# A gated mix of a long convolution and a routed row update on one core: second products of the fine shifts left unsummed, transform differences as accumulating transfers, and a new written-out order

## The chip, the cores and the metric

The kernel runs on one core of one Trainium2 chip. The metric is the device time of one execution in microseconds. An execution is profiled separately; its times are in us from the first instruction unless marked ns. The engines are PE (TensorE matmul; PEld is its weight load), DVE (VectorE), ACT (ScalarE), POOL (GpSimd) and SP (SyncE, which here only issues transfers).

## The reference, cut to what matters

With x of shape (1, 2048, 512) the output is g * a + (1 - g) * b, where g is a sigmoid of one dot product per row.

```python
# a: a long convolution along the 2048 rows, one kernel K per channel
logdA = dt * (A_re + 1j * A_im)                      # 512 channels x 128 states
P = jnp.exp(logdA[:, :, None] * l[None, None, :])    # l = arange(2048) in bfloat16
K = jnp.einsum("dn,dnl,dn->dl", Cc, P, dt * Bc).real
y = irfft(rfft(pad(u)) * rfft(pad(K)))[:2048] + u * Dskip
# b: the two rows of x with the largest x @ w_r go through a small gated MLP,
#    are scaled by a sigmoid and added back to x at their place
```

The lags `l` are rounded to bfloat16, so that far fewer than 2048 different ones occur; the kernel evaluates K at 32 x 20 of them.

## The kernel before, in words

**Lag kernel K.** A lag is written as a coarse part (32 values, `T1`) plus a fine part (20 values, `T2`). For each half `hf` (or `c`) of 256 channels, `coarse(hf)` makes the complex powers exp(logdA * T1), 128 states on the partitions, in tiles `TP`: `phases` makes angles as matmuls on PE (`pa`), ACT turns them to sines and cosines (`sin`), `ns` negates one of them, and two multiplies on DVE (`pi`, `pr`) join them with the decays (`ep`, exponentials on ACT). `fine(hf)` makes the 20 fine powers, weighted by C * dt * B, in `X` (in the region `TQ`): a complex product is two real multiplies, `px` and `py`, and an add, `ps`. For fine shifts 8 to 15 the second products `py` are not added: they lie in `Y`, and PE adds them. For shifts 0 to 7 and 16 to 19 there is a scratch tile (`t4`) and the add `ps` on DVE. `lags(c)` contracts over the states: 64 groups of four channels, each with two parts (real, imaginary); per group and part one matmul of 80 columns (20 shifts x 4 channels, from `X`) and one of 32 columns (8 shifts x 4 channels, from `Y`) into the same PSUM columns 32 to 63 (`kmm`, lines 889 and 890). `kae` copies PSUM to SBUF, `sel` (matmuls of a selection matrix) reorders, `kce`, `kcx` and `k0c` fill `KC`, and `kt` and `ku` make a small tail term. Before these, the weights come from `np` (DVE), `nw` (PE), `kw` (DVE), `wx`, `wp`, `wn`.

**Transforms.** The convolution is done by a cosine and sine transform of each block of 1024 rows. `transform(m)` for block m: for each plane pl (cosine, sine), eight 128x512 products per tile (`fw`), the odd rows first (`fwo`, stored doubled as 2 * odd in V[1]) and then odd plus even (`fwe`, stored in V[0]); `vb` on DVE then makes V[1] = V[0] - V[1], that is even minus odd, one TENSOR_TENSOR of 128x2048 per block and plane. `spectrum(c, i)` makes the transform of K (`ks` on PE, `khe` on ACT). `products(c, j)` multiplies both (`prod`, then `yr`, `yi`, `pq` or PE sums `ac` with `ace`, then `b0` to `b13`), `inverse(c, j)` goes back (`iv` on PE, `ive` on ACT or DVE with the gate as scale, and `out`).

**Rows.** `log` (64 small matmuls on a transposed copy of x, `xt`, loaded by a DMA transpose that occupies SP's queue) gives g and the router's values; `gm`, `gt`, `gm2` find two maxima; `gu` gathers their rows, `ff`, `dn`, `zt`, `z1`, `bu` make the update; `uc` copies x to a DRAM tensor and `sc` scatters the two rows into it; `ue` and `u2` load from there what `inverse` adds. `rd` makes diagonal matrices for that.

**Order.** The program records operations with what they read and write (`P.add`); each may have alternatives on two engines. `PLAN` is a list of (operation number, alternative) written out by hand: it gives every engine its instructions in order, and with them the waits. `BANKS` gives each PSUM tile its bank. An engine runs its list strictly in order. SP's list is a DMA queue; POOL's too, for the few transfers that it issues.

The bookkeeping of buffers matters to the change: a writer waits for all readers of whatever lay at its place before.

## Time and profile before

| what | value |
|---|---|
| time, median of 3 runs | 158.11 us (157.82 to 158.44) |
| time of the profiled execution | 159.26 us, its span 157.2 us |
| mean granted clock of PE | 0.991 |
| busy: PE, DVE, ACT, POOL | 140.8, 137.9, 119.0, 21.0 us |
| instructions: PE, DVE, ACT, POOL | 1622, 184, 177, 26 |
| HBM traffic | 19.78 MB read, 4.20 MB written |

The profiled execution is 2.1 us longer than its span, which is what lies around the first and the last instruction. Engines overlap, so busy times do not add up to the span; what an engine waited for is read from the rows with an idle time before them. The end of a matmul in the profile includes its way through the array, some 0.16 us; the pace of a run of matmuls is read from their starts. A line such as L386 is a helper's (all TENSOR_TENSORs have it); L402 and L408 are PSUM evictions on ACT and DVE, L411 the other ACT functions, L716 is `fw`, L930 and L932 `ks`, L903 `sel`, L1131 `rd`, L618 and L620 the phase products, L548 `nw`, L653 `log`.

### The profile page before, as it was taken

The page shows a single profiled execution, that of the slowest core. Times are in us where ns is not written, and L with a number is a line of the kernel's source. Part 1 is how long each engine was busy: PE and PEld are TensorE (multiplying, and loading weights), DVE is VectorE, ACT ScalarE, POOL GpSimd, SP SyncE. Part 2 cuts the span into 40 slices and gives each one's busy share as a digit, 9 for nine tenths or more (in the row PEclk, how much of TensorE's full clock was granted, in tenths as well). Part 3 has the DMA queues.
Part 4 walks back from the last instruction along what each step waited for, and adds up shares of the span by engine and source line. Part 5 has one row for each costly group of instructions (what it writes and reads, how often), then busy time and mean ns, then how long its engine had stood idle before and what let it go on. Part 6 is the DMA issues. An engine that isn't in the chain of part 4 may idle for free.

```text
span 157.2 us, 3769 instructions
## 1 busy us (share of the span) xinstructions
PE 140.8 (90%) x1622; PEld 103.5 (66%) x1635; DVE 137.9 (88%) x184; ACT 119.0 (76%) x177; POOL 21.0 (13%) x26
## 2 busy tenths in 40 slices
PE   2479998999998999999967999999999999999960
PEld 0259976444764555778636899668877767777850
DVE  0799689999998999999999999999987999996930
ACT  5699999999999898887982754758687963567820
POOL 5000011564508800002020000000000000000000
PEclk9999999999999999999999999999999999999996
DMA  3999999968399000340397500558000040000157
GB/s 84 216 245 272 314 424 409 407 233 254 103 364 559 17 0 4 81 190 1 65 363 259 152 8 4 179 163 264 15 4 0 0 133 0 6 0 0 33 159 212
DMA packets 20932, 24.35 MB, mean 155 GB/s; under 512 B 9358, under 2 KB 18068, under 8 KB 20244
## 3 DMA queue, kind: packets, MB, share of 16 engines
q1 hardware_dynamic: 20642, 23.97, 47.3%
q8 instruction: 13, 0.21, 0.6%
q10 hardware_dynamic: 146, 0.13, 0.3%
q0 software_dynamic: 128, 0.01, 0.2%
q14 instruction: 3, 0.02, 0.0%
HBM read 19.78 MB, written 4.20 MB: 153 GB/s over the span
## 4 chain that ended last, share of the span: by engine, by line
PE 53%; DVE 32%; issue 4%; POOL 3%; ACT 2%; DMA 1%; POOLq 1%; ACTq 0%
DVE RB L386 23%; PE psm L930 9%; PE psm L1076 9%; PE psm L993 5%; PE psm L889 4%; PE psm L995 3%; PE psm L548 3%; PE psm L997 3%; PE psm L932 2%; PE psm L1071 2%; POOL RB L396 2%; PE psm L935 2%; DVE RB L726 2%; DVE RB L408 2%; PE psm L598 2%
## 5 line engine op out<-in xcount | busy, mean ns | idle before, releaser
L386 DVE TENSOR_TENSOR RB<-RB 128x2048 bf16<-128x2048 bf16 (+5 forms) x112 | 110.0, 1033 | 2.4 <-ACT RB L402 1.1
L402 ACT ACTIVATE RB<-psm 128x1024 bf16<-128x1024 f32 (+5 forms) x54 | 49.1, 945 | 23.7 <-PE psm L997 10.0
L716 PE MATMUL psm<-RB 128*128 128x512 bf16 x121 | 28.8, 379 | 1.2 <-ACT RB L402 0.5
L411 ACT ACTIVATE RB<-RB 128x512 bf16<-128x512 f32 (+6 forms) x48 | 27.0, 644 | 1.7 <-DVE RB L386 1.5
L411 ACT ACTIVATE RB<-psm 128x1024 bf16<-128x1024 int16 (+2 forms) x23 | 21.6, 968 | 2.5 <-DVE RB L386 1.2
L716 PEld LDWEIGHTS psm<-RB 128*128 128x128 bf16 x128 | 11.7, 97 | 14.0 <-ACT RB L402 1.1
L1076 PE MATMUL psm<-RB 128*128 128x256 bf16 x128 | 18.9, 273 | 0.0
L889 PE MATMUL psm<-RB 128*128 128x80 bf16 x256 | 16.5, 197 | 0.0
L890 PE MATMUL psm<-RB 128*128 128x32 bf16 x256 | 16.4, 177 | 0.0
L889 PEld LDWEIGHTS psm<-RB 128*128 128x128 bf16 x256 | 16.1, 96 | 0.2
L890 PEld LDWEIGHTS psm<-RB 128*128 128x128 bf16 x256 | 16.0, 96 | 0.2
L930 PE MATMUL psm<-RB 128*128 128x256 bf16 x128 | 14.5, 273 | 1.5 <-ACT RB L402 1.5
L930 PEld LDWEIGHTS psm<-RB 128*128 128x128 bf16 x128 | 12.4, 98 | 3.9 <-ACT RB L402 2.1
L1076 PEld LDWEIGHTS psm<-RB 128*128 128x128 bf16 x128 | 12.5, 98 | 1.5
L408 DVE CAST RB<-psm 128x1024 bf16<-128x1024 f32 (+3 forms) x8 | 8.6, 1080 | 3.7 <-PE psm L548 1.7
L993 PE MATMUL psm<-RB 128*128 128x512 bf16 x35 | 11.3, 379 | 0.3
L1087 ACT ACTIVATE RB<-psm,RB 128x256 bf16<-128x256 f32 x25 | 9.8, 477 | 1.3 <-PE psm L1076 1.1
L396 POOL CAST RB<-RB 128x16 bf16<-128x16 f32 (+4 forms) x6 | 7.2, 1197 | 24.8 <-DVE RB L405 16.9
L618 PE MATMUL psm<-RB 128*128 128x256 f16 x64 | 9.0, 272 | 0.0
L1071 PE MATMUL psm<-RB 128*128 128x256 bf16 x32 | 8.7, 273 | 0.0
L995 PE MATMUL psm<-RB 128*128 128x256 bf16 x40 | 8.3, 272 | 0.1
L997 PE MATMUL psm<-RB 128*128 128x256 bf16 x40 | 8.3, 273 | 0.0
(74 smaller groups left out, 156.9 us busy)
## 6 DMA issues: line engine op xcount, KB each, us to landing
RB<-c_fwd SPq DMA_DIRECT2D x2, 1024.0 KB, 7.9
RB<-in_A_u_dram SPq DMA_DIRECT2D x2, 1024.0 KB, 6.8
RB<-c_near SPq DMA_DIRECT2D x2, 1024.0 KB, 5.2
RB<-u_routed SPq DMA_DIRECT2D x2, 1024.0 KB, 5.1
RB<-in_B_w_up_dram SPq DMA_DIRECT2D x1, 1792.0 KB, 10.4
RB<-in_B_w_gate_dram SPq DMA_DIRECT2D x1, 1792.0 KB, 14.4
RB<-in_B_w_down_dram SPq DMA_DIRECT2D x1, 1792.0 KB, 8.7
out_dram<-RB SPq DMA_DIRECT2D x6, 256.0 KB, 3.0
```

The costliest lines, as they stand in the source:

```text
L386: return P.add(name, [(eng, c_dve(n, mode) if eng == DVE else 1.6, lambda h: h.tensor_tensor(out=o(), in0=a_(), in1=b_(), op=op))], rd, wr ...
L402: return lambda h: h.activation(out=o(), in_=a_(), func=ACTF.Copy, scale=scale() if callable(scale) else scale)
L411: return P.add(name, [(ACT, cost or c_act(n), lambda h: h.activation(out=o(), in_=a_(), func=func, scale=scale))], rd, wr, table=table, **kw)
L716: x = h.matmul(P32(t, k2, 0, 128, 0, (1, 512)), FM(0, 128, pl * 4096 + (par * 4 + i) * 512 + (2 * kp + k2) * 128, (1, 128)), U(0, 128, ((m ...
L889: h.matmul(P32(t, q // 6, 0, 128, (q % 6) * 80, (1, 80)), tp, TQv(0, 128, c * 10240 + ri * NT2 * 256 + r * 4, (256, NT2), (1, 4)), start=( ...
L890: x = h.matmul(P32(t, q // 6, 0, 128, (q % 6) * 80 + 32, (1, 32)), tp, ARENA(0, 128, eY[c] + ri * 2048 + r * 4, (256, 8), (1, 4)), start=F ...
L930: x = h.matmul(o, KN(0, 128, g * 2048 + col, (1, 128)), KC[c](0, 128, g * 256, (1, 256)), start=(g == 0), stop=(g == NG - 1))
L993: r = h.matmul(P32(t, kt, 0, 128, 0, (1, 512)), CI(0, 128, 0, (1, 128)), f(k, 0, 512), start=(k == 0 and hc == 1), stop=False, skip_group_ ...
L995: r = h.matmul(P32(t, kt, 0, 128, 256, (1, 256)), CI(0, 128, 0, (1, 128)), f(k, 0, 256), start=False, stop=False, skip_group_check=True)
L997: r = h.matmul(P32(t, kt, 0, 128, 0, (1, 256)), NEG(0, 128, 0, (1, 128)), f(k, 1, 256), start=False, stop=(k == od[-1]), skip_group_check= ...
L1071: h.matmul(o, RD(0, 128, (tb + 8) % 16 * 128, (1, 128)), UE[q](0, 128, r * 256, (1, 256)) if early else U2(0, 128, tb * D + c * CW, (1, 25 ...
L1076: x = h.matmul(o, G(0, 128, (pl * 2 + kt // 2) * 1024 + (r * 2 + q) * 128, (1, 128)), PQ(0, 128, r * 1024 + kt * 256 + pl * 256 if quarter ...
```

## The change: what it does

1. **`fine`.** The adds `ps` of shifts 4 to 7 and of 16 to 19 are gone. Their second products are written to `Y`, which now holds 16 shifts (4 to 19) in two pieces per part, instead of 8. `py` for shifts 8 to 15 becomes two multiplies of 128x2048 instead of one of 128x4096. The add of shifts 0 to 3 stays.
2. **`lags`.** The second matmul has 64 columns (16 shifts x 4 channels) instead of 32, into PSUM columns 16 to 79.
3. **`transform`.** Odd rows are stored as -2 * odd. `vb` is no longer a DVE instruction: it is two DMAs with accumulation, issued by POOL (`ACC`), that add V[0] to V[1], 128 x 2 x 512 values (256 KB) each; four such pairs in all.
4. **Small things.** `ldt` (log_dt) is loaded from SP's queue, ahead of all, instead of ACT's. The tile `neg` gets a place of its own. In program order `products(0, 0)` and `inverse(0, 0)` come after `lags(1)`.
5. **`PLAN` and `BANKS`** are new. What moves, read from the new list against the old one:

| engine | before | after |
|---|---|---|
| SP, start | cia, ldn, nat1, nat3, nat4, dga, nat5, dsr, nat2, xt, cf, dgb, fm1, u0, fm0 | ldt, cia, nat1, dgb, ldn, dga, nat5, dsr, xt, nat4, nat2, nat3, cf, u0, fm1, fm0 |
| SP, later | kt (half 0), u8, ue, tm, u2, ue, kt (half 1), u2 | u8, ue, ue, u2, kt (half 1), u2, kt (half 0), tm |
| PE, start | phases of qargs0 and weights, nw, log, phases of coarse0 | phases of coarse0, weights, qargs1, qargs0, log, coarse0; nw after the second gt |
| PE, middle | coarse1 phases between fw of both blocks, lags0, sel, four ks, lags1 | the same, with other fw; zt after sel; five ks before lags1 |
| DVE, start | args mixed with np, kw, wx, then rows and gm | all args, log and gm, np between the gm steps, kw after powers |
| DVE, from fine1 on | rest of fine1, vb, vb, prod, prod, yi, kae, vb, yr, pq, kce, ... vb | rest of fine1, prod, bu, prod, yr, yi, kae, pq, pq, kce, khe, ... |
| DVE, new there | | three ns, two khe, rd of block 0 (from ACT); dtn |
| ACT, before sel | ..., neg, ..., k0c, kae, kae, rd, then kcx, kce | ..., kae, kae, k0c, kcx, kce, then rd of block 1 |
| ACT, later | rd of block 1 between ace; last ive of inverse(1,1) on DVE | z1 after four khe; last ive of inverse(1,1) on ACT |
| POOL | ..., sgo, rsf, sgd, sgo, gsil, hh, sc, rr | ..., rr, gsil, hh, sgd, vb (block 0, plane 1), sgo, vb (block 1, plane 1), vb (block 0, plane 0), rsf, vb (block 1, plane 0), sc |

The diff, without the two lists:

```diff
+        def ACC(name, vs, rd, wr, kb):
+            return P.add(name, [(POOL, 1.5 * len(vs), lambda h: [h.dma_start(out=o(), in_=a_(), accum_op=ALU.add) for o, a_ in vs])], rd, wr, dma=(4.0, kb / 100.0, len(vs)))
...
+        NEG, bNEG = small("neg", 256, BF)
...
-        DMA("ldt", ..., eng=ACT, first=2900.0, lat=2.0)
+        DMA("ldt", ..., first=2900.0, lat=2.0)
...
-                    P.add("fwo", [(ACT, c_act(1024), f_act(o, a, 2.0)), (DVE, ... scalar1=2.0 ...)], [t], [bVO[m][pl]])
+                    P.add("fwo", [(ACT, c_act(1024), f_act(o, a, -2.0)), (DVE, ... scalar1=-2.0 ...)], [t], [bVO[m][pl]])
...
-                v = lambda hc, pl=pl: (lambda: V(0, 128, vo[m][0] + (hc * 2 + pl) * 512, (vo[m][2] - vo[m][0], 2), (2048, 2), (1, 512)))
-                TT("vb", v(1), v(0), v(1), ALU.subtract, [bV[m][0][pl], bVO[m][pl]], [bV[m][1][pl]], 2048)
+                v = lambda hc, z, pl=pl: (lambda: V(0, 128, vo[m][2 * z] + (hc * 2 + pl) * 512, (2048, 2), (1, 512)))
+                ACC("vb", [(v(1, z), v(0, z)) for z in range(2)], [bV[m][0][pl], bVO[m][pl]], [bV[m][1][pl]], 512)
...
-        YR = [("V", 16384), ("TQ", 8192)]
+        YR = [((("V", 16384), ("V", 20480)), (("A", 22528), ("S", 2048))), ((("TQ", 8192), ("TQ", 12288)), (("A", 22528), ("TQ", 16384)))]
...
+            y = lambda b_, ri: Y[ri][b_ // 2] + 1024 * (b_ % 2)
+            y2 = lambda b_: ap(y(b_, 0), (y(b_, 1) - y(b_, 0), 2), (256, 4), (1, 256))
             for k, (j0, b0) in enumerate(((0, 4), (4, 0))):
-                bt = bf_("t%d_%d" % (j0, hf), "A", 22528, 4096)
+                bt = bY[hf][0] if k else bf_("t%d_%d" % (j0, hf), "A", 22528, 4096)
+                o_ = y2(0) if k else t4
                 TT("px", x(j0, 4), ...)
-                TT("py", t4, ...)
-                TT("ps", x(j0, 4), x(j0, 4), t4, ALU.add, [bx[k], bt], [bx[k]], 2048)
+                TT("py", o_, ...)
                 if k == 0:
+                    TT("ps", x(j0, 4), x(j0, 4), t4, ALU.add, [bx[k], bt], [bx[k]], 2048)
...
-            TT("py", ap(Y, (2048, 2), (256, 8), (1, 256)), ap(N, (X - N, 2), (0, 8), (1, 256)), ..., [bY[hf]], 4096)
+            for ri in range(2):
+                TT("py", ap(y(1, ri), (y(2, ri) - y(1, ri), 2), (256, 4), (1, 256)), ap(X if ri else N, (0, 8), (1, 256)), ..., [bY[hf][1 + ri]], 2048)
             TT("px", x(16, 4), ...)
-            TT("py", t4, x(0, 4, 1, -5120), ..., [bt], 2048)
-            TT("ps", x(16, 4), x(16, 4), t4, ALU.add, [bx[3], bt], [bx[3]], 2048)
+            TT("py", y2(3), x(0, 4, 1, -5120), ..., [bY[hf][3]], 2048)
...
-                                x = h.matmul(P32(t, q // 6, 0, 128, (q % 6) * 80 + 32, (1, 32)), tp, ARENA(0, 128, eY[c] + ri * 2048 + r * 4, (256, 8), (1, 4)), ...)
+                                x = h.matmul(P32(t, q // 6, 0, 128, (q % 6) * 80 + 16, (1, 64)), tp, ARENA(0, 128, eY[c][ri][0] + r * 4, (eY[c][ri][1] - eY[c][ri][0], 2), (256, 8), (1, 4)), ...)
...
-        inverse(0, 0, products(0, 0))
         fine(1)
         residual(1)
         lags(1)
+        inverse(0, 0, products(0, 0))
```

More of the change, by code (lines that the diff above doesn't have):

```diff
@@ L472, in bass_gated_mix__ssm_conv_s4__moe_arch_mod__prompt_kernel @@
         prm = [A_A_re, A_A_im, A_B_re, A_B_im, A_C_re, A_C_im]
-        DMA("ldt", lambda h: [h.dma_start(LDT(0, 1, 0, (1, D)), dr(A_log_dt, 0, (D, 1), (1, D)))], [], [bLDT], 1, eng=ACT, first=2900.0, lat=2.0)
+        DMA("ldt", lambda h: [h.dma_start(LDT(0, 1, 0, (1, D)), dr(A_log_dt, 0, (D, 1), (1, D)))], [], [bLDT], 1, first=2900.0, lat=2.0)
         DMA("cia", lambda h: [h.dma_start(CI(0, 128, 0, (1, 128)), dr(id_c, 0, (512, 128), (1, 128)))], [], [bCIA], 32, eng=SP, first=2900.0)
@@ L725, in store @@
                 else:
[L726 removed]
+                    P.add("fwo", [(ACT, c_act(1024), f_act(o, a, -2.0)), (DVE, c_dve(1024, 1), lambda h: h.tensor_scalar(out=o(), in0=a(), scalar1=-2.0, scalar2=None, op0=ALU.mult))], [t], [bVO[m][pl]])
             return product, store
```

25 lines of the change are left out of this document (12 added, 13 removed), and 64 rows, old and new, of the table PLAN.

## The prediction

> **What bounds the kernel now.** I read the shares of the engines first, then the busy time by stage, then the chain and single rows. The page's shares of the engines, the chain's shares, and busy time in six stages up to PE's end (stretch, length, busy us and count of PE, PEld, DVE, ACT, POOL, then clock, DMA share, GB/s):
>
> ```profile
> PE 140.8 (90%) x1622; PEld 103.5 (66%) x1635; DVE 137.9 (88%) x184; ACT 119.0 (76%) x177; POOL 21.0 (13%) x26
> PE 53%; DVE 32%; issue 4%; POOL 3%; ACT 2%; DMA 1%; POOLq 1%; ACTq 0%
> 0.00:20.00 20.00, 13.76 (x128) 11.23 (x129) 13.16 (x31) 16.29 (x25) 2.25 (x8) 1.00 0.93 229
> 20.00:65.00 45.00, 42.98 (x393) 25.25 (x398) 43.27 (x64) 43.45 (x61) 16.62 (x17) 1.00 0.63 239
> 65.00:79.40 14.40, 13.38 (x291) 11.19 (x292) 14.19 (x16) 12.27 (x16) 1.73 (x2) 1.00 0.35 109
> 79.40:83.60 4.20, 2.68 (x48) 1.42 (x48) 4.10 (x5) 3.63 (x10) 0.43 (x1) 1.00 1.00 375
> 83.60:114.00 30.40, 30.39 (x473) 25.79 (x474) 29.52 (x27) 18.07 (x21) 0.00 (x0) 1.00 0.40 122
> 114.00:152.00 38.00, 37.66 (x296) 28.64 (x298) 33.00 (x45) 25.30 (x47) 0.00 (x0) 1.00 0.09 26
> ```
>
> The reader is to see that PE, not DVE, has the least room. From 83.60 to 152.00 PE stands still 0.35 us of 68.4. From 20 to 83.6 it stands still 2.02 + 1.02 + 1.52 = 4.6 us, and DVE and ACT are as full as PE there (1.7 and 1.6 us idle in 20 to 65). The change removes no PE work. So it can win only what PE waits for: those 4.9 us, and part of the 6.2 us before 20. The chain's 32% on DVE says that DVE leads somewhere, not that its time is worth as much at the end.
>
> Where DVE hands over to PE (rows of both engines; start, length, then what ended the idle time before):
>
> ```profile
> 60.50 2.29 DVE L386 TENSOR_TENSOR RB<-RB 128x4096 bf16<-128x4096 bf16 x1
> 65.23 0.20 PE L889 MATMUL psm<-RB 128*128 128x80 bf16 x1
> 78.31 0.18 PE L890 MATMUL psm<-RB 128*128 128x32 bf16 x1
> 79.40 2.68 PE L903 MATMUL psm<-RB 128*32 128x128 bf16 x48 [0.91 <-ACT RB L402]
> 79.86 2.45 ACT L1131 ACTIVATE RB<-RB 128x128 bf16<-128x128 bf16 x8 [0.52 <-POOL RB L386]
> 82.34 1.22 ACT L402 ACTIVATE RB<-psm 32x512 bf16<-32x512 f32 x2
> 83.61 0.61 PE L930 MATMUL psm<-RB 128*128 128x256 bf16 x4 [1.53 <-ACT RB L402]
> 87.62 2.29 DVE L386 TENSOR_TENSOR RB<-RB 128x4096 bf16<-128x4096 bf16 x1
> 89.82 2.35 DVE L386 TENSOR_TENSOR RB<-RB 128x2048 bf16<-128x2048 bf16 x2
> 90.61 0.20 PE L889 MATMUL psm<-RB 128*128 128x80 bf16 x1
> ```
>
> The last operand of `lags0` is done at 62.79, PE comes to it at 65.23: 2.4 us spare. The last of `lags1` is done at 89.91, PE comes at 90.61: 0.7 us spare. The two `vb` of `transform0` follow at 89.82.
>
> **The change part by part.**
>
> *Sums dropped in `fine`* (two `ps` per half). Each is a 128x2048 TENSOR_TENSOR as in the row at 89.82, two in 2.35 us, or 1.15 each: 4 x 1.15 = 4.6 us less DVE. Two stand before 62.79, where PE came 2.4 us later anyway; two before 89.91, where it came 0.7 us later. On the end: 0 by themselves. They are the cover for PE coming earlier. Cutting `py` of 4096 in two costs some 0.1 us of DVE per half, covered.
>
> *Differences `vb` as transfers*: another 4.6 us less DVE. The first pair stands behind `fine1`, before the first `prod`; PE has `lags1` and `spectrum0` to do then and waits 0.01 us in that stage. On the end: 0, provided that they land in time (below).
>
> *Wider second product.* 256 matmuls go from 32 to 64 columns:
>
> ```profile
> 66.72 0.60 PE L620 MATMUL psm<-RB 128*128 128x256 f16 x4
> 39.27 1.54 PE L779 MATMUL psm<-RB 128*128 128x2 bf16 x56
> ```
>
> 24 pairs run from 65.23 to 66.72, 62 ns a pair. 56 matmuls of two columns take (1.54 - 0.16)/55 = 25 ns each, so narrow ones pay a floor of 25, and the 80-column partner the other 37. Bounds for 64 columns: 25 (nothing) and 37 (256 x 12 = 3.1 us). A straight line from 25 ns at 32 columns to 37 at 80 gives 33 at 64, or 2.0 us. But 37/80 is 0.46 ns a column, and by that the floor reaches to 54 columns and 64 take 29.6: I take 256 x 4.5 = 1.1 us more, all of it on PE, half before `sel` and half in `lags1`. The Trainium skill (TensorE: Matmul & The Clock Gate, "Wait — 56ns, not 53.3ns?") gives a warm pitch of columns/2.4 GHz + 2.5 ns, never under 25: an estimate of 29.2 ns and 1.1 us in all, against 2.0 by the straight line, which would end at 157.9 instead of 157.0; the trace agrees at 2 columns, no run here shows 64.
>
> *Start.* `ldt` leaves ACT's queue, so A_re is issued first there:
>
> ```profile
> 0.72 0.52 ACTq L473 DMA_DIRECT2D RB<-in_A_log_dt_dram  x1
> 1.27 0.37 ACTq L476 DMA_DIRECT2D RB<-in_A_A_re_dram  x1
> 4.78 9.09 SPq L420 DMA_TRANSPOSE RB<-in_A_u_dram  x1
> RB<-in_A_u_dram SPq DMA_TRANSPOSE x1, 11.2
> 12.52 4.59 PE L548 MATMUL psm<-RB 128*128 128x128 f32 x32
> 15.83 1.28 PE L548 MATMUL psm<-RB 128*128 128x128 f32 x10
> 17.16 2.26 PE L653 MATMUL psm<-RB 128*128 128x2 bf16 x64
> 19.29 0.38 PE L618 MATMUL psm<-RB 128*128 128x256 f16 x2
> 20.59 0.61 PE L599 MATMUL psm<-RB 128*128 128x256 f16 x4
> 17.15 1.23 DVE L408 CAST RB<-psm 128x1024 bf16<-128x1024 f32 x1 [1.70 <-PE psm L548]
> L399 DVE SCALAR_TENSOR_TENSOR RB<-RB 128x256 f32<-128x256 bf16 x8 | 3.6, 477 | 0.0
> ```
>
> A_re comes 0.55 us earlier; A_im stays third on SP, so I take -0.4 for all that hangs on both (bounds 0 and -0.55). The transpose `xt` moves one place up SP (-0.4) and three `nat` loads move behind its 9.09 us. They then land near 18, and so `np` and `nw` move behind `log`. `log` now begins at 4.4 + 11.2 = 15.6 and ends at 17.9 (19.4 before). PE then still owes `nw`: 32 at the pace of its last ten, 0.11 us, 3.6 us (the 4.59 has a slow head). It has done two other phase products instead, 1.3 us each by the stretch from 19.29 to 20.59. So it is 1.5 us earlier with 1.0 us more to do; I take -0.2, since the first products of a cold PE are slow in any order (bounds -0.5 and +0.5). DVE, though, stands from about 12 to 18. By 18.4 it had done eight `np` (3.6 us) and `kw` (1.2); now they come after, and it is some 4 us behind, net of the small row operations that it does first. With two `ps` fewer (2.3) and the start's 0.4 its last operand for `lags0` comes at 62.8 + 4 - 2.3 - 0.4 = 64.1, if its 1.7 us of waits in 20 to 65 stay: still ahead of PE, but by little.
>
> *ACT lighter.* All three `ns` of ACT (1.05 us each) go to DVE, `z1` and one `rd` (2.45) go behind `sel`, the other `rd` to DVE:
>
> ```profile
> L402 ACT ACTIVATE RB<-RB 128x1024 bf16<-128x1024 bf16 x3 | 3.2, 1054 | 0.1
> ACT RB L402 <- PE psm L997: 10.0, 8, 2.4
> ```
>
> In 65 to 83.6 PE waits for ACT (the 0.91 and 1.53 above); before, its waits are many and short, and I take ACT, which empties PSUM, as the likeliest releaser. With 3.2 + 2.5 us less work for it I let PE win 1.3 of the 3.0 us that it stands still in 20 to 79.4 (bounds 0 and -3.0; what brings them back is a rival below). The 0.9 before `sel` and the 1.22 of `kcx` and `kce` after it stay; `rd` ends at 82.31, `sel` at 82.08, so its removal gives -0.2. After `sel` DVE gets `rd` and two `khe`, some 3.5 us; `vb` and `ps` gave it 6.8 there, and ACT's longest wait for PE, 10.0 us in all, shows that ACT had room.
>
> *Products of channel half 0 after `lags1`* in program order: in the old written-out order they already ran about there, so nothing moves by it but the banks. 114 to 152: DVE lighter, -0.2 of the 0.34. `ive` for the last tile on ACT instead of DVE: +0.1.
>
> *The transfers.* On POOL they stand behind `sgd`, in the order transform0 plane 1, transform1 plane 1, transform0 plane 0, `rsf`, transform1 plane 0, then the scatter `sc`. The second waits for ACT's eviction of transform1, in the old run at 67.4, in the new order behind one more sine, near 72; all behind it wait too: plane 0, which the first `prod` (near 89) needs, and `rsf`, which `z1` on ACT needs near 90.
>
> ```profile
> 66.42 1.01 ACT L402 ACTIVATE RB<-psm 128x1024 bf16<-128x1024 f32 x1
> 72.92 1.07 POOL L812 DMA_INDIRECT u_routed<-RB  x1 [18.30 <-DVE RB L386]
> u_routed<-RB POOLq DMA_INDIRECT x1, 4.2
> out_dram<-RB SPq DMA_DIRECT2D x6, 256.0 KB, 3.0
> RB<-RB SPq DMA_DIRECT2D x2, 48.0 KB, 3.5
> L396 POOL CAST RB<-RB 128x1 bf16<-128x1 f32 x1 | 3.3, 3307 | 5.1 <-DVE RB L663 5.1
> 46.69 3.40 DVE L386 TENSOR_TENSOR RB<-RB 128x4096 bf16<-128x4096 bf16 x2
> ```
>
> No row shows an accumulating transfer. Issue: 1.07 us to 3.3 (POOL's slowest row, one element). Landing of 256 KB: 3.0 us to 3.5 x 256/48 = 18.7. Nearest are POOL's own: 1.07 and 4.2. So 72 + 4 x 1.07 + 4.2 = 80.5, 8 us before `prod`: cost 0. The far end, 72 + 13.2 + 18.7 = 104, costs 13 us, since one `kae` of `lags1` stands on DVE behind four of these products and `sel` waits for it: two of 2.29 and two of 1.15 take DVE from 89 to 96, PE's ten groups of 12 pairs (66 ns) take it from about 89.5 to 97.5, so DVE has 1.5 to 2 us to spare, until about 91. `sc` now goes out after `bu` near 92 rather than 73 and lands near 97; on SP's queue `ue` waits for it, and behind `ue` stand `u2`, both `kt`, `tm` and the first `out`. All but `out` land by about 110, and their reader, `iv` of half 0, runs in the last stage, after 114: covered.
>
> **Sum**: start -0.4, order up to `log` -0.2, PE's waits -1.3, `rd` -0.2, width +1.1, last stage -0.2 and +0.1 = -1.1. The profiled execution took 159.26 us for a span of 157.2 (so some 158.2 is due), and the median of the runs shown is 158.11, 1.15 below it; taken off the median: 157.0 us.
>
> **The rivals.**
>
> *Slower: the transfers land late.* What speaks for it: POOL's one-element cast took 3.3 us while DVE ran multiplies for 3.4. If each issue costs 3.3 and the landing doubles to 8.4, plane 0 lands at 72 + 13.2 + 8.4 = 93.6, 2.6 us past 91; from 1.1 us late on it eats the whole gain. It gives 158.11 - 1.1 + 2.6 = 159.6. Against it: the 1.07 us row also lies under a busy DVE. Beside it, the Trainium skill (SBUF — State Buffer, "SBUF: two separate sides") says that a transfer issued by GpSimd has its descriptors written by that engine, which a VectorE instruction in a two-port mode locks out; the 3.3 us row may be of that kind; no run here shows it for a transfer.
>
> *Slower: DVE's idle stretch from 12 to 18.* If the `nat` loads land 2 us past 18, `np` waits, and behind it on DVE every eviction of transform0 that frees a bank for PE's next `fw`; `lags0`, whose last operand comes at 64.1 by the sum above, is late by some 2.5: 158.11 - 1.1 + 2.5 = 159.5. It decides from 1.1 us on. Against it: `cf`, which leaves SP right behind the transpose now, delayed nothing.
>
> *No change*: PE's waits in 20 to 79.4 come back elsewhere: 158.11 - 1.1 + 1.3 = 158.3. For it: DVE and ACT are 96% full there and the order is as tight as before.
>
> *More*: nearly all waits from 20 to 83.6 go, another -1.7 (the rest of the 3.0): 155.3. Against: `kcx` and `kce` still follow `sel`.
>
> **How the numbers follow.** Likeliest 157.0, chance 0.48, its own range 156.0 to 158.0. No change 0.20, more 0.11, late transfers 0.12, early DVE 0.09. A change under 0.5% (0.8 us) can't be told from none here; of the likeliest case's own range some seven tenths lie beyond it. So faster 0.34 + 0.11 = 0.45, same 0.14 + 0.20 = 0.34, slower 0.12 + 0.09 = 0.21. Range 155.0 to 160.0: it takes in every case above; the 18.7 us landing, some 170, lies outside.
>
> **What would show it.** PE's first `kmm` near 64.5 and `sel` near 78; kmm pairs near 66 ns; the first phase product near 8.3; DVE with a gap before `log`, some 128 to 131 us busy, and new gaps after 90; POOL issues near 72 to 77 of about 1 us each. Wrong, if a pair takes over 70 ns, if the first `prod` waits for a DMA, or if PE idles over 3 us between 20 and 65.

## The result and the profile after

The changed kernel takes 157.85 us, median of 20 runs (156.42 to 158.69); the kernel before takes 158.54 beside it, median of 20 (157.82 to 159.66). The ratio is 0.9935, 95% interval 0.9909 to 0.9961: 1.0 us less (0.6 to 1.4). The medians differ by 0.7, the means (157.55 and 158.57) by 1.0, since the runs of the changed kernel lie in two groups. 157.0 was predicted. Runs more than 1.5% above the fastest of their kernel are left out of the ratios, not of the medians. The groups are eight runs from 156.42 to 157.12 and twelve from 157.65 to 158.69 (median 158.02), with nothing between. The profiled execution, 156.56 us with a span of 154.8, is of the lower group, 1.3 us under the median, so its trace is not the typical case; what may part the groups comes below.

The profile after: the shares of the engines, the chain, and busy time by stage (columns as before):

```profile
PE 141.0 (91%) x1635; PEld 103.7 (67%) x1635; DVE 132.9 (86%) x181; ACT 114.1 (74%) x168; POOL 28.7 (19%) x34
...
PE 63%; DVE 25%; DMA 5%; SPq 1%; ACT 1%; issue 1%; ACTq 0%; DVEq 0%
...
0.00:20.00 20.00, 13.51 (x134) 9.93 (x135) 9.64 (x28) 16.32 (x26) 2.68 (x9) 1.00 0.88 222
20.00:65.00 45.00, 44.60 (x443) 27.79 (x441) 44.67 (x66) 42.27 (x60) 14.31 (x16) 1.00 0.80 277
...
79.40:83.60 4.20, 2.66 (x31) 2.15 (x24) 4.20 (x6) 3.71 (x11) 1.03 (x1) 1.00 1.06 283
83.60:114.00 30.40, 30.25 (x464) 24.95 (x462) 27.82 (x27) 19.46 (x22) 2.74 (x1) 1.00 0.48 127
```

PE does the same work (141.0 us against 140.8), DVE 5.0 us less. From 20 to 65 PE stands still 0.40 us, where it stood 2.02. DVE had 1.7 us idle in that stretch and has 0.3 now: the shorter list of DVE was spent at once on an order in which PE arrives earlier.

The hand-overs, in the order of those shown of before (rows of PE, DVE and ACT):

```profile
59.58 3.50 DVE L386 TENSOR_TENSOR RB<-RB 128x2048 bf16<-128x2048 bf16 x3
63.13 0.10 PEld L897 LDWEIGHTS psm<-RB 128*128 128x128 bf16 x1 [0.27 <-DVE RB L386]
74.86 0.19 PE L898 MATMUL psm<-RB 128*128 128x64 bf16 x1
...
75.83 0.19 PE L898 MATMUL psm<-RB 128*128 128x64 bf16 x1
77.09 2.68 PE L911 MATMUL psm<-RB 128*32 128x128 bf16 x48 [1.06 <-ACT RB L402]
80.33 0.95 DVE L408 CAST RB<-psm 128x768 bf16<-128x768 f32 x1
81.53 2.67 PE L938 MATMUL psm<-RB 128*128 128x256 bf16 x23 [1.54 <-DVE RB L408]
89.43 0.20 PE L897 MATMUL psm<-RB 128*128 128x80 bf16 x1
```

`lags0` starts at 63.13 instead of 65.23, and PE now waits for DVE there (before, DVE was 2.4 us early). `sel` starts at 77.09 instead of 79.40. The gap ahead of the spectrum is as long as it was, 1.54, but the releaser is another: `kce` on DVE, which stands behind three operations of `fine1` and starts at 80.33 though `sel` ends at 79.77. Fifteen pairs from 74.86 to 75.83 make 65 ns a pair.

The start, first of the kernel before, then of the changed kernel (ACT's wait for the small load; DVE; PE's phase products; `log`):

```profile
8.71 0.61 PE L598 MATMUL psm<-RB 128*128 128x256 f16 x2 [3.16 <-DVE RB L386]
```

```profile
5.62 3.85 ACT L411 ACTIVATE RB<-RB 128x4 bf16<-128x4 bf16 x8 [2.07 <-DMA RB<-in_A_log_dt_dram]
5.86 0.17 DVE L405 CAST RB<-RB 128x4 f32<-128x4 bf16 x1 [1.04 <-ACT RB L411]
9.05 0.61 PE L622 MATMUL psm<-RB 128*128 128x256 f16 x2 [3.90 <-DVE RB L386]
10.94 0.63 PE L622 MATMUL psm<-RB 128*128 128x256 f16 x2
13.14 0.38 PE L602 MATMUL psm<-RB 128*128 128x256 f16 x2
15.11 2.27 PE L657 MATMUL psm<-RB 128*128 128x2 bf16 x64
17.41 0.19 DVE L405 COPY RB<-psm 128x32 f32<-128x32 f32 x1 [4.93 <-PE psm L657]
```

`dtn` (the CAST at 5.86) now stands on DVE between `al` and `bs`. It waits for `dth` on ACT, that for the load of log_dt, which lands at 5.6; so `bs` and all behind it come later, and the first phase product starts at 9.05, 0.34 later than before. The two rows of the same kind at 10.94 and 13.14 show PE's speed: 0.63 us for two matmuls, then 0.38; start to start these are 213 and 107 ns.

The end (SP's output transfers and the last multiply on an output), before and after:

```profile
149.52 3.96 SPq L1099 DMA_DIRECT2D out_dram<-RB  x4
152.01 0.69 DVE L1091 TENSOR_TENSOR RB<-psm,RB 128x512 bf16<-128x512 f32 x1 [0.51 <-PE psm L1076]
153.52 0.81 SPq L1095 DMA_DIRECT2D out_dram<-RB  x1
```

```profile
150.25 1.22 SPq L1107 DMA_DIRECT2D out_dram<-RB  x2
150.73 0.84 ACT L1095 ACTIVATE RB<-psm,RB 128x256 bf16<-128x256 f32 x2 [2.46 <-PE psm L1084]
151.59 0.56 SPq L1103 DMA_DIRECT2D out_dram<-RB  x1
```

Before, the last output was ready at 152.70 but SP was still issuing four others until 153.48; from the end of the last multiply to the end of the span 4.5 us passed. Now it is issued at once, and 3.2 us pass.

The transfers (group, transfer; the `ns` multiply on DVE, whose mean was 416 ns before):

```profile
L420 POOL DMA_DIRECT2D RB<-RB x8 | 10.3, 2305 | 3.8 <-ACT RB L402 3.8
RB<-RB POOLq DMA_DIRECT2D x8, 256.0 KB, 8.9
L629 DVE TENSOR_SCALAR RB<-RB 128x1024 bf16<-128x1024 bf16 x8 | 4.2, 520 | 0.5 <-ACT RB L411 0.4
```

Eight issues keep POOL busy for 10.3 us, 1.29 each (single rows overlap, hence the mean of 2.3), and a transfer lands 8.9 us after its issue, twice the 4.2 assumed. Still no `prod` waits: the first starts at 89.20, right behind `fine1`.

Another wait for a load is new. `ku` on DVE, a small multiply, reads what `kt` brings (DVE's row):

```profile
108.10 4.83 DVE L386 TENSOR_TENSOR RB<-RB 128x256 bf16<-128x256 bf16 x5 [0.83 <-DMA RB<-RB]
```

DVE has no such wait in the profile before. There the parts of `kt` land 3.4 to 3.6 us after their issue; now they take 3.9 to 5.9. More loads run beside them (the DMA engines' share from 104 to 110 is 0.92, where it was 0.62), but that this is the cause is not shown. DVE also comes to `ku` sooner without the differences; with these back on DVE (below) its profile has no such wait.

### The profile page after: what moved, and what is told of

Read it like the earlier page. It is cut to its first block, busy times and chain, and to the rows that moved or that the text cites. A ratio compares the mean times of both kernels' runs of the same rounds, so it can differ in the third digit from the quotient of the medians.

```text
span 154.8 us, 3775 instructions
## 1 busy us (share of the span) xinstructions
PE 141.0 (91%) x1635; PEld 103.7 (67%) x1635; DVE 132.9 (86%) x181; ACT 114.1 (74%) x168; POOL 28.7 (19%) x34
## 4 chain that ended last, share of the span: by engine, by line
PE 63%; DVE 25%; DMA 5%; SPq 1%; ACT 1%; issue 1%; ACTq 0%; DVEq 0%
DVE RB L386 17%; PE psm L720 17%; PE psm L1084 7%; PE psm L897 5%; PE psm L622 5%; PE psm L938 5%; PE psm L898 4%; PE psm L1001 4%; DMA RB<-RB 3%; DVE RB L399 3%; PE psm L624 3%; DVE RB L408 2%; DMA RB<-in_A_log_dt_dram 2%; PE psm L783 2%; PE psm L911 2%; PE psm L1079 2%
## 5 line engine op out<-in xcount | busy, mean ns | idle before, releaser
L386 DVE TENSOR_TENSOR RB<-RB 128x2048 bf16<-128x2048 bf16 (+7 forms) x106 | 101.0, 1001 | 2.2 <-DMA RB<-RB 0.8
L402 ACT ACTIVATE RB<-psm 128x1024 bf16<-128x1024 f32 (+5 forms) x52 | 47.8, 942 | 25.1 <-PE psm L1005 10.3
L720 PE MATMUL psm<-RB 128*128 128x512 bf16 x128 | 29.3, 379 | 0.0
L720 PEld LDWEIGHTS psm<-RB 128*128 128x128 bf16 x128 | 12.2, 98 | 13.3 <-ACT RB L411 0.2
L1084 PE MATMUL psm<-RB 128*128 128x256 bf16 x128 | 18.9, 273 | 0.0
L897 PEld LDWEIGHTS psm<-RB 128*128 128x128 bf16 x256 | 16.9, 96 | 0.7 <-issue 0.3
L897 PE MATMUL psm<-RB 128*128 128x80 bf16 x256 | 17.4, 198 | 0.0
L898 PE MATMUL psm<-RB 128*128 128x64 bf16 x256 | 17.4, 191 | 0.0
L898 PEld LDWEIGHTS psm<-RB 128*128 128x128 bf16 x256 | 16.9, 97 | 0.0
L938 PE MATMUL psm<-RB 128*128 128x256 bf16 x128 | 14.3, 273 | 1.5 <-DVE RB L408 1.5
L1095 ACT ACTIVATE RB<-psm,RB 128x256 bf16<-128x256 f32 x28 | 11.2, 477 | 5.2 <-PE psm L1084 5.1
L938 PEld LDWEIGHTS psm<-RB 128*128 128x128 bf16 x128 | 12.4, 98 | 3.4 <-issue 1.7
L1084 PEld LDWEIGHTS psm<-RB 128*128 128x128 bf16 x128 | 12.5, 98 | 1.5
L408 DVE CAST RB<-psm 128x1024 bf16<-128x1024 f32 (+3 forms) x10 | 11.0, 1105 | 2.4 <-PE psm L898 1.1
L1001 PE MATMUL psm<-RB 128*128 128x512 bf16 x40 | 12.6, 380 | 0.2
L420 POOL DMA_DIRECT2D RB<-RB x8 | 10.3, 2305 | 3.8 <-ACT RB L402 3.8
L622 PEld LDWEIGHTS psm<-RB 128*128 128x128 f16 x64 | 6.3, 103 | 6.1 <-DVE RB L386 4.4
L1079 PE MATMUL psm<-RB 128*128 128x256 bf16 x32 | 8.7, 273 | 0.0
```

Source lines behind the costliest of these rows:

```text
L386: return P.add(name, [(eng, c_dve(n, mode) if eng == DVE else 1.6, lambda h: h.tensor_tensor(out=o(), in0=a_(), in1=b_(), op=op))], rd, wr ...
L402: return lambda h: h.activation(out=o(), in_=a_(), func=ACTF.Copy, scale=scale() if callable(scale) else scale)
L408: return P.add(name, [(ACT, 0.10 + n * 0.83e-3, f_act(o, a_)), (DVE, 0.15 + n * 1.04e-3, lambda h: h.tensor_copy(o(), a_()))], rd, wr, **kw)
L622: r = h.matmul(o, DGM(0, 128, d * 128, (1, 128)), HL(0, 128, z * 512 + hf * CW, (1, CW)), start=(u == 0 and z == 0 and i % 2 == 0), stop=F ...
L720: x = h.matmul(P32(t, k2, 0, 128, 0, (1, 512)), FM(0, 128, pl * 4096 + (par * 4 + i) * 512 + (2 * kp + k2) * 128, (1, 128)), U(0, 128, ((m ...
L897: h.matmul(P32(t, q // 6, 0, 128, (q % 6) * 80, (1, 80)), tp, TQv(0, 128, c * 10240 + ri * NT2 * 256 + r * 4, (256, NT2), (1, 4)), start=( ...
```

## The experiments

Times of different batches are compared through their ratios to the kernel before, which ran beside each; the half-widths of two ratios are combined as the root of their squares. The upper group of the changed kernel alone lies at 0.9968 of the kernel before (means, 158.07 to 158.57).

**Width alone, in the old order.** In the kernel before, one argument of the second lag product:

```
- ..., 0, 128, (q % 6) * 80 + 32, (1, 32)), tp, ARENA(..., (256, 8), (1, 4))
+ ..., 0, 128, (q % 6) * 80 + 16, (1, 64)), tp, ARENA(..., (0, 2), (256, 8), (1, 4))
```

> The kernel before, with nothing changed but the second product of a lag pair, 64 columns instead of 32 (its 32 columns of `y` read twice, so the lag sums get terms that don't belong). It prices the width alone, in the old order, with all sums still on DVE. Theory (TensorE is the bound from 65 to 83.6 and in lags1, so width is paid in full): pairs go from 62 to 65.4-66.5 ns, 256 pairs cost 0.9 to 1.1 us, the time is 0.6 to 1.3 us above the kernel before. Rival (the waits for DVE and ACT around the lags take the width up): pairs as wide, but the time is within 0.3 us of the kernel before.

Measured: 159.63 us, ratio to the kernel before 1.0058 (1.0026 to 1.0090): 0.9 us more (0.4 to 1.4). The groups of the two lag products, of the kernel before and of this one:

```profile
L889 PE MATMUL psm<-RB 128*128 128x80 bf16 x256 | 16.5, 197 | 0.0
L890 PE MATMUL psm<-RB 128*128 128x32 bf16 x256 | 16.4, 177 | 0.0
```

```profile
L889 PE MATMUL psm<-RB 128*128 128x80 bf16 x256 | 17.4, 198 | 0.0
L890 PE MATMUL psm<-RB 128*128 128x64 bf16 x256 | 17.3, 191 | 0.0
```

The 256 pairs take 17.4 us instead of 16.5. That is the 0.9, and the end moves by all of it: PE is the bound there, as predicted.

**Transfers alone, in the old order.** In the kernel before, `vb` as accumulating transfers (and `fwo` scaled by -2), three of the four behind `hh` on POOL, one behind `rr`:

```
- TT("vb", v(1), v(0), v(1), ALU.subtract, ...)
+ ACC("vb", [(v(1, z), v(0, z)) for z in range(2)], ...)
```

> The kernel before, with nothing changed but the four `vb`: eight accumulating transfers on POOL, in the gaps of POOL's old queue (three of them behind `hh`, so from about 55 us, the fourth behind `rr`). Theory of the prediction (DVE's time there is covered): within 0.3 us of the kernel before; the two `vb` between 89.8 and 92.1 go, the first `prod` starts near 90, and what DVE gains stands as idle time in front of `kae` or later. Rival (DVE leads in lags1 and after, so 2.3 us less ahead of `kae` are worth something): 0.5 to 1.2 us below the kernel before. Second rival (POOL's issues and their hold on the SBUF port cost DVE): 0.5 us or more above it, with DVE's `ns` or `pi` during the issues longer by 0.4 us each.

Measured: 159.14 us, ratio 1.0024 (0.9995 to 1.0052): 0.4 us more (-0.1 to +0.8). DVE loses 4.3 us of work (137.9 to 133.6) and nothing is won. Not as expected, the first `prod` does not start near 90: it waits for ACT (DVE's row of this kernel):

```profile
91.93 5.75 DVE L386 TENSOR_TENSOR RB<-RB 128x4096 bf16<-128x4096 bf16 x3 [2.15 <-ACT RB L402]
```

So in the old order the two `vb` ahead of `prod` filled a wait. They were free there. The second rival is not excluded: the interval reaches past 0.5, and one `ns` on DVE took 0.70 us during the issues, instead of 0.42.

**Differences back on DVE, in the new order.** The changed kernel with the old `vb`, two ahead of the first `prod`, two ahead of the first `prod` of the other half:

```
- ACC("vb", ...)   # POOL, behind sgd
+ TT("vb", v(1), v(0), v(1), ALU.subtract, ...)   # DVE
```

> The changed kernel, with the four differences back on DVE as one subtraction each: transform0's two just ahead of the first `prod`, transform1's two just ahead of the first `prod` of the other channel half. Theory (in the new order DVE has 1.06 us idle before `kae` and 0.8 before `ku`): the first pair pushes `kae` of lags1 by 2.3 - 1.1 = 1.2 us, `sel` of lags1 by about as much, less what ACT holds it for; the time is 0.3 to 1.2 us above the changed kernel. The prediction's pricing of the transfers at nothing would hold with a time within 0.3 us of the changed kernel. Rival (the transfers cost the port and DMA time): below it by 0.3 us or more.

Measured: 159.78 us, ratio 1.0066 (1.0041 to 1.0090); against the changed kernel 1.0066/0.9935 = 1.0132, half-width 0.0036: 2.1 us more (1.5 to 2.6), above the range that I gave. PE's weight loads ahead of `sel` of `lags1` and of the first of the accumulated products:

```profile
100.78 2.16 PEld L911 LDWEIGHTS psm<-RB 128*32 128x32 bf16 x48 [1.67 <-ACT RB L402]
...
116.53 0.13 PEld L1001 LDWEIGHTS psm<-RB 128*128 128x128 bf16 x2 [2.09 <-ACT RB L402]
```

In the changed kernel these loads wait 0.49 and 0.61 us. Both pairs of `vb` push PE, by 1.2 and 1.5 us. The releaser in brackets is the last by the profile; DVE's `kae`, which ends at 100.67 behind the `vb`, is the one that comes later than before. What was free in the old order is not in the new one. All eight runs lie between 159.46 and 160.01; against the upper group of the changed kernel alone they are 1.6 us longer (1.0066/0.9968), still above the range.

**Sums back on DVE, narrow product, in the new order.** The changed kernel with

```
+ TT("ps", x(j0, 4), x(j0, 4), o_, ALU.add, ...)      # for both k
+ TT("ps", x(16, 4), x(16, 4), y2(3), ALU.add, ...)
- second product: 64 columns
+ second product: 32 columns
```

> The changed kernel, with the four `ps` back on DVE and the second product of 32 columns, the same sums as before; order and transfers as in the changed kernel. Theory (dropping the sums was needed as cover for the new order): PE saves 0.9 us of width, but the last operand of lags0 comes 2.3 us later than 63.1 where PE waits already, and lags1's 2.3 us later than 89.3; with 0.45 us of width given back on each side the time is 1.5 to 3.5 us above the changed kernel. Rival (the sums are worth nothing and the width costs): 0.5 to 1.0 us below the changed kernel.

Measured: 162.63 us, ratio 1.0239 (1.0201 to 1.0276); against the changed kernel 1.0306, half-width 0.0046: 4.8 us more (4.1 to 5.6), again above the range. PE's first pair of `lags0` and of `lags1`, and two windows behind the latter:

```profile
66.69 0.21 PE L899 MATMUL psm<-RB 128*128 128x80 bf16 x1 [1.26 <-DVE RB L387]
...
95.00 0.20 PE L899 MATMUL psm<-RB 128*128 128x80 bf16 x1 [2.41 <-DVE RB L387]
...
95.00:98.00 3.00, 3.00 (x78) 3.00 (x79) 3.00 (x3) 0.97 (x1) 0.29 (x1) 0.71 0.02 5
98.00:101.00 3.00, 3.00 (x83) 3.00 (x81) 2.97 (x3) 0.21 (x1) 2.45 (x1) 0.72 0.00 0
```

The restored `ps` show as PE waiting for DVE, and there is more: after the stand of 2.41 us ahead of `lags1` the granted clock is 0.71 and 0.72 in the next two windows. The stand is paid twice: 6 us at that clock lose some 1.7 us of work (an estimate from the two windows).

**Around `sel`.** In the changed kernel's written-out order:

```
- kmm 286, kae 287 | kmm 283, kmm 284, kae 285 | px, ps, kce
+ kmm 283, kmm 284, kae 285 | kmm 286, kae 287 | px, kce, ps
```

> The changed kernel, with two moves around `sel` of lags0: the one-bank group of lag pairs (`kmm` 286, evicted in 0.44 us) goes last instead of the two-bank group (0.97 us), so that the last eviction before `sel` is the short one; and `kce` on DVE goes ahead of one `ps` of fine1. Theory (PE stands still 1.19 us before `sel` for ACT and 1.70 us before `ks` for DVE's `kce`, which is queued behind fine1's operations): the gap before `sel` falls to about 0.7, the one before `ks` to about 1.4, 0.5 to 0.8 us in all, and the time is 0.4 to 0.8 us below the changed kernel, unless fine1's last operand (89.28, PE waits 0.35 for it already) then holds PE. Rival (that one holds: DVE, not PE's gaps, sets when lags1 starts): both gaps shrink, the gap before lags1 grows by as much, and the time is within 0.3 us of the changed kernel.

Measured: 158.37 us, ratio 0.9978 (0.9950 to 1.0005); against the changed kernel 1.0043, half-width 0.0038: 0.7 us more (0.1 to 1.3), 0.2 against the upper group alone. The gain did not come, and the rival's mechanism holds. DVE's `kce`, PE's spectrum and first pair of `lags1`:

```profile
81.04 0.96 DVE L408 CAST RB<-psm 128x768 bf16<-128x768 f32 x1 [0.65 <-PE psm L911]
...
82.36 7.15 PE L938 MATMUL psm<-RB 128*128 128x256 bf16 x64 [1.16 <-ACT RB L402]
...
91.42 0.20 PE L897 MATMUL psm<-RB 128*128 128x80 bf16 x1 [1.04 <-DVE RB L386]
```

PE's wait ahead of the spectrum falls from 1.54 to 1.16, but DVE stands 0.65 us for `sel`, `fine1` ends that much later, and PE's weight loads wait 1.51 us ahead of `lags1`, where they waited 0.35. Nor does the order of the evictions help: ACT does four of them without a break (75.22 to 78.25), whichever comes last.

**The start.** In the changed kernel, `dtn` behind `lo`; and, in the first of the two kernels, `xt` also two places up on SP:

```
- al, dtn, bs, bn, bn2, hi, lo          # DVE
+ al, bs, bn, bn2, hi, lo, dtn
- dga, nat5, dsr, xt                    # SP, s_start alone
+ dga, xt, nat5, dsr
```

> The changed kernel, with `dtn` on DVE moved behind `lo`, so that `bs` no longer waits for `dth` and the small load of log_dt, and the transposing load `xt` ahead of `nat5` and `dsr` on SP. Theory (the prediction's -0.4 for the start was lost to this wait): the first phase product starts at 8.3 instead of 9.04, `xt` lands near 14.1, `log` starts 0.7 us earlier and the time is 0.4 to 0.9 us below the changed kernel. Rival (TensorE's slow first microseconds set the start of `log`, so where its first product lies matters less than when it speeds up): first product at 8.3 as well, but `log` and the time move by less than 0.3 us, or by as much either way as the two groups of the changed kernel lie apart.

> The changed kernel with `dtn` moved behind `lo` on DVE, and `xt` left where it is: one half of `s_start`. Theory (`log` waits for PE's slow phase products, which start 0.8 us earlier; `xt`, landed at 14.95, holds it only where TensorE speeds up early): most of the gain of `s_start` remains, the median is 156.6 to 157.2. Rival (the load `xt` made the gain): within 0.3 us of the changed kernel, 157.85.

Measured: with both, 156.47 us, ratio 0.9856 (0.9822 to 0.9891), against the changed kernel 0.9920, half-width 0.0043: 1.3 us less (0.6 to 1.9). With `dtn` alone, 156.82 us, ratio 0.9872 (0.9831 to 0.9913): 1.0 us less (0.2 to 1.8). The first phase product starts at 8.26 and 8.46 in the two profiles. So the wait of `bs` cost about 1 us; what the load adds is not resolved (the two ratios differ by 0.0016, half-width 0.0054). The first has the lowest ratio here, 2.3 us under the kernel before (0.0144 x 158.5).

**When PE speeds up.** In the trace of the kernel with the differences on DVE, whose start is that of the changed kernel, PE's phase products read:

```profile
8.94 0.61 PE L622 MATMUL psm<-RB 128*128 128x256 f16 x2 [4.04 <-DVE RB L386]
...
14.04 0.64 PE L602 MATMUL psm<-RB 128*128 128x256 f16 x2
...
15.14 0.38 PE L602 MATMUL psm<-RB 128*128 128x256 f16 x2
```

Two matmuls still take 0.64 at 14.04, where the changed kernel's profile had 0.38 from 12.5 on. PE speeds up 6 us after its first phase product instead of 3, `log` starts (by its first weight load) at 16.35 instead of 15.04, and the first lag pair comes at 64.34 instead of 63.13. The other two profiles with the changed kernel's start and without `dtn` moved are of this kind too (`log` at 16.10 and 16.23). The 1.2 us are about the distance between the two groups of runs (1.3 by their medians). That the groups are these two cases is an inference from four profiles; the other runs have none.

A second thing varies, and it can move a run as far. The profile with `dtn` and `xt` both moved is of the slowest run of that kernel (157.62 us; the other six 155.87 to 156.52), though its `log` starts early, at 15.19. It loses its time later, at `ku` on DVE and then at the first accumulated product on PE:

```profile
109.16 4.83 DVE L386 TENSOR_TENSOR RB<-RB 128x256 bf16<-128x256 bf16 x5 [1.67 <-DMA RB<-RB]
...
114.35 0.38 PE L1001 MATMUL psm<-RB 128*128 128x512 bf16 x1 [1.21 <-ACT RB L402]
```

The bracket names the last releaser by the profile; but PE's weight load there starts 0.12 us after the five multiplies of DVE end (113.99), as it does in the changed kernel's profile (112.93). From its first product in `sel` of `lags1` to its last product, PE takes 52.73 us here. It takes 51.57 to 51.62 in the three profiles of the new order in which `ku` waits 0.43 to 0.56 us, and 51.88 in that of the changed kernel (0.83). So this wait made the run some 1.1 us longer, and the two groups may come from it as well as from PE's speed.

To take the late speed-up away I filled PE's wait with dummy matmuls, first inside the two parameter products:

```
+ for _ in range({0: 1, 1: 10}[i]):
+     r = h.matmul(<free bank>, CI(0, 128, 0, (1, 128)), NAT(0, 128, i * 512, (1, 512)), ...)
```

> The changed kernel, with eleven dummy matmuls (128x128 by 512 columns, into a PSUM bank that nobody reads) on TensorE: one behind the first parameter product, ten behind the second, in the 4.3 us in which it waits for the phases' operands. Nothing else moves. Theory (the changed order put the `log` product behind four phase products; these run at 213 ns per 256 columns until TensorE speeds up to 107, which came 3.1 us after the first of them in the profile of 156.56 us and 5.9 us after it in the profile of the kernel with the differences on DVE, and that is why the runs of the changed kernel lie in two groups, around 156.7 and 158.1): the phase products run fast from the first or from soon after, `log` starts no later than 15.1 in every run (it can't start before `xt` has landed near 14.95), and the median goes from 157.85 to 156.5-157.0 with a smaller spread. Rival (the groups come from when `xt` lands): no change of the median beyond 0.3 us, PE waits for the DMA ahead of `log`.

> The kernel before, with eight such dummy matmuls behind its second parameter product. Theory (the old order has the `nw` products, not the `log` product, where TensorE is still slow, and `xt` lands at 16.0, so `log` can come forward by 0.9 us at most): 0.3 to 0.9 us below the kernel before. Rival (the slow start costs both orders the same): 1.1 to 1.5 us below it, as in the changed kernel.

The kernel before with them is slower: 160.85 us, ratio 1.0142 (1.0099 to 1.0184), 2.3 us more. The changed kernel with them has no ratio: of six runs two took 156.82 and 157.17 us, at a mean granted clock of 1.00 and 0.99, and four 159.79 to 161.04, at 0.975 to 0.978. `bs` waits for the operation that the dummies are in, so they delayed it: a fault of the experiment. It still shows the speed. PE's first phase product in the changed kernel with dummies, and windows of the kernel before with dummies:

```profile
11.04 0.39 PE L624 MATMUL psm<-RB 128*128 128x256 f16 x2 [3.16 <-DVE RB L386]
```

```profile
10.00:12.00 2.00, 0.01 (x1) 0.02 (x2) 1.90 (x5) 2.00 (x5) 0.00 (x0) 1.00 1.28 290
12.00:14.00 2.00, 2.00 (x12) 1.47 (x13) 2.00 (x8) 1.98 (x4) 0.00 (x0) 0.59 1.28 290
14.00:16.00 2.00, 2.00 (x9) 1.30 (x8) 2.00 (x6) 0.80 (x2) 0.00 (x0) 0.56 1.14 220
```

In the first, PE stood 3.16 us and was fast from its first product on (0.39 for two). In the second it stood until 11.98, 3.16 us by its row too, and fell back to 0.59 and 0.56 of its clock. The same stand lost the speed in one and not in the other. The first profile is of the run of 156.82 us; none of the four long runs has one, so what happened in them is not shown.

Then as operations of their own, on top of `s_start`:

```
+ MM("warm", <8 matmuls of 512 columns>, [bCIA, bNAT[0]], [], ...)   # behind nt1
+ MM("warm", <8 matmuls of 512 columns>, ...)                        # ahead of log, g_warm_fill alone
```

> The kernel of `s_start`, with two groups of eight dummy matmuls (512 columns each, into a bank that nobody reads) as operations of their own, for which nobody waits: one behind the second parameter product (PE waits 3.6 us there), one behind the last of the four phase products, ahead of `log`. Theory (in `e_warm` the dummies were inside the operation for which `bs` waits, so `bs` came 1.9 us late and PE stood 3.65 us, in which it fell back to 213 ns per 256 columns in four of six runs; without that fault the phase products run fast from 8.3): phase products of 1.2, 0.4, 1.4 and 1.3 us end near 12.6 at the latest, `log` starts when `xt` has landed, near 14.4 instead of 15.2, and the median is 155.4 to 156.0, against 156.47 for `s_start`. Rival (DVE, not `log`, sets the rest of the first half): `log` as early, but the time within 0.3 us of `s_start`.

> The same with the first group alone. Theory: PE ends its phase products near 11.6 to 12.6 and stands some 2 to 2.8 us for `xt`; a stand of 2.87 us cost half speed for 3.8 us in the kernel with the sums back on DVE, so `log` and what follows run slow in a part of the runs: the median lies 0.3 to 1.5 us above `g_warm_fill`, with a larger spread and a granted clock under 0.99 in the slower runs. Rival (a stand of that length does no harm here): the same as `g_warm_fill` within 0.3 us.

Measured: 157.20 us, ratio 0.9872 (0.9823 to 0.9922), and 157.23 us, ratio 0.9891 (0.9844 to 0.9937). Against `s_start` the first is 1.0016, half-width 0.0060: no gain. The phase products did run fast, from 8.4 to 12.9, and `log` started at 14.5 in both, 0.7 earlier than in the profile of `s_start`. But the second group made no difference either, and the gain went here (window of the kernel with one group):

```profile
18.00:20.00 2.00, 2.00 (x10) 1.33 (x9) 1.78 (x6) 1.65 (x2) 0.35 (x1) 0.50 0.98 375
```

Right after `log`, 64 products of two columns, the clock is at half, with PE counted busy throughout: the speed that PE had from 8.41 on was lost again. PE had stood 1.38 us ahead of `log` here, but the kernel with both groups, which fills that wait, shows 0.50 in the same stretch too, and the kernel with `dtn` alone moved, which has no dummies, 0.53. The changed kernel has the same 64 products, and its profile shows 1.00. What decides it is not shown, nor how often it happens in runs without a profile.

**Order of the outputs alone.** In the kernel before, one entry moved:

```
- out 524, out 527, out 520, out 441, out 482, out 522    # SP
+ out 441, out 524, out 527, out 520, out 482, out 522
```

> The kernel before, with one transfer moved: the two output transfers of inverse01 (ready at 145.81) go ahead of the first single-row output on SP, as they do in the changed kernel, instead of behind all three, where they issue with two others in one stretch of 3.96 us that ends at 153.48 and holds the last output back from 152.70. Theory (the 1.3 us that the changed kernel wins between its last multiply on an output and the end comes from SP's queue, and is a gain of the order of the outputs, not of what DVE or TensorE save): the last output is issued near 152.8, the stretch from the end of the last multiply to the end of the span falls from 4.5 to 3.2-3.6 us, and the time is 0.7 to 1.3 us below the kernel before. Rival (the same bytes have to drain, so the end is set by the DMA engines): within 0.3 us of the kernel before.

Measured: 158.18 us against 158.40, ratio 0.9981 (0.9951 to 1.0011): 0.3 us less, anywhere from 0.8 less to 0.2 more. SP's rows:

```profile
150.91 1.23 SPq L1099 DMA_DIRECT2D out_dram<-RB  x2
152.19 0.64 SPq L1095 DMA_DIRECT2D out_dram<-RB  x1
```

The stretch from the last multiply (ends 152.02) to the end of the span (155.5) is 3.5 us, as the theory had it, where four profiles of the old order have 4.0 to 4.6, and all nine of the new one 3.2. The timing shows a third of the expected 1 us and does not exclude zero. The trace says that the order of the outputs shortens the end; how much of the time it is worth stays open.

## Why the prediction was right, and where it was not

The sign and the size came out: 1.0 us less by the ratio, 1.1 predicted; 157.85 lies 0.85 above the 157.0, within the likeliest case's own range, and the kernel before lay 0.4 higher here (158.54) than the 158.11 it was counted from. Term by term:

- *Bound.* PE as the bound holds: the width of 256 products was paid in full in the old order (0.9 us), and taking 4.3 us off DVE there was worth nothing.
- *Width*, +1.1 by 4.5 ns a pair: 3.5 ns (16.5 to 17.4 us), +0.9. The guess that the 25 ns floor ends near 54 columns was nearer than the straight line (2.0).
- *Sums and transfers, "0 by themselves", the cover for PE coming earlier*: right as worded, but I gave the cover no price. It is 2.1 us for the differences. For the sums it is 4.8, net of the width that the narrow product saves, and some 1.7 of that is the lost clock. The sums were not dropped alone in the old order, so their "0 by themselves" is not tested. The working said what each part costs when it is there, not what the new order costs when it is missing.
- *PE's waits, -1.3 of 3.0*: from 20 to 65 alone PE's idle time fell by 1.6. The releaser that I named, ACT, is not shown to be the one that mattered: with DVE's work put back, PE waited for DVE in `lags0` and `lags1` and, as I read the rows, ahead of `sel` and of the accumulated products. No run gives ACT its work back, so what its lighter list won stays open.
- *Start, -0.4*: failed. The parameter load did come earlier and `al` started 0.6 earlier, but I did not follow `dtn`, which moved to DVE between `al` and `bs`, behind a load that lands at 5.6. The first product came 0.34 later, by the two profiles; the mistake is worth 1.0 us (0.2 to 1.8).
- *Order up to `log`, -0.2*: the size was off, by the point I had noted and not priced, that the first products are slow. `log` came 1.9 us earlier in one profile and 0.6 to 0.85 in three others, by when PE sped up. And the profile that I counted from is the latest of its kind: by the first weight load `log` starts at 16.95 there and at 16.21, 16.27 and 16.77 in three other profiles with the old start, so three of the four of the changed start (16.10 to 16.35) gained little or nothing.
- *`rd`, -0.2*: failed. The place was right, but `kce` on DVE took over as the last to finish, and the gap stayed 1.54. Moving it only moved the wait.
- *Transfers late*: the landing was 8.9 instead of 4.2, the issue 1.29 instead of 1.07; both inside the bounds, and the cover up to 89 was enough. What failed is "covered" for the loads behind `sc`: I took `iv` of half 0 for the reader of them all, but `ku` on DVE reads `kt` already at 108.1, and waits 0.83 us for it in the changed kernel's profile and 1.67 in another.
- *Last stage, +0.1 for `ive` on ACT*: the wrong sign. I priced the multiply and did not look at SP's queue; the end of the span is 1.3 us shorter in the profile. By the profiles most of that is the order of the outputs; the timing shows 0.3 of it and leaves the rest open.
- *DVE's idle stretch from 12 to 18*: it came (4.93 us), and `lags0` was then late by 0.27 only.
- *No change* (0.2 us more by its sum) and *More* (2.8 less) both lie outside the measured 0.6 to 1.4 less. From 20 to 83.6 PE stands still 3.0 us in this profile, where it stood 4.6.

Of what I said would show it: `sel` near 78 (77.09), pairs near 66 ns (65) and the gap before `log` are there; the first phase product at 8.3 is not (9.05), nor the first `kmm` at 64.5 (63.13, earlier; 64.34 and 64.40 in two profiles in which PE speeds up late). Six issues of POOL stand from 72.7 to 80.4, but two came at 55.5 already, and DVE's 132.9 us lie above my 128 to 131. The sum was right partly by luck: by the profile, which is of the lower group, I had the start 0.7 us too short and the end 1.4 too long, and left the wait for `kt` out.

## What to carry to other kernels

Slack on a second engine has no price by itself: the four differences on DVE cost nothing under one order and 2.1 us under the next, because a tighter order has spent the slack; so price a part in the order in which it will run. When an instruction moves between engines, walk everything that it waits for and everything queued behind it there, even for one of 128x4 elements. When a transfer moves to a later time, look for the first instruction that reads what it brings, on every engine. And look at the queue that issues the last transfers before pricing the last computation.

## What was not expected of the hardware

- PE's first products ran at 213 ns per 256 columns and later at 107. The change came 3.0 to 6.0 us after the first phase product, differently in runs of the same start, while the recorded granted clock was 1.00 throughout; the record shows only later falls. The Trainium skill (TensorE: Matmul & The Clock Gate, "Part 1: The HAM clock gate (the "warmup" mystery)") says that PE starts at half clock and is released after a window of some 3.4 us of activity, which runs free of the kernel's start; the traces agree with the two rates and with a moment that varies. That section of the Trainium skill gives it as some 500 ns either way; the spread here is 3 us.
- The clock fell back after stands of 2.41 us (to 0.71 and 0.72 over two windows of 3 us) and 3.16 us (0.59 over 2), not after one of 3.16 in another profile, and also with PE counted busy, after 64 products of two columns (0.50 to 0.53 from 18 to 20 us in three profiles; 1.00 in the changed kernel's). The same section of the Trainium skill gives an idle window of some 3.4 us for the fall; by the matmul rows none of these stands was that long (by the weight loads the two of 3.16 read 3.65 and 4.06).
- While POOL issued the transfers, `ns` on DVE took 0.78 and 0.80 us where it met them. In the kernel with the differences on DVE the same two took 0.41 and 0.42; the mean of eight is 520 ns against 429 (row below). The TENSOR_TENSORs beside it kept their 1.22 us. By the Trainium skill (SBUF — State Buffer, "SBUF: two separate sides") a two-port operation of VectorE and GpSimd exclude each other on a shared port; the prediction feared that for POOL, and it is DVE that was seen to pay, 0.7 us in all. That the port is the cause is not shown.

```profile
L629 DVE TENSOR_SCALAR RB<-RB 128x1024 bf16<-128x1024 bf16 x8 | 3.4, 429 | 0.6 <-ACT RB L411 0.6
```
